# Sparse attention followed by a gated MLP: transposes of the first batch on TensorE, the spatial weight transposed by DMA one batch later

## The chip, the cores and the metric

The kernel runs on one core of one Trainium2 chip. The metric is the device time in microseconds, as the median of the runs. One execution is also recorded by the hardware profiler; where and when below refer to that recording. PE is TensorE, ACT is ScalarE, DVE is VectorE, Pool is GpSimd, and SP is the engine from whose queue nearly all DMAs of this kernel are issued. A queue is worked off in the order of the program.

## What is computed

The reference has two parts. First, block-sparse attention over 4 batches, 8 heads, 768 positions and 64 dimensions a head. Then the heads are put side by side (768 x 512 for each batch) and go through a gated MLP that mixes positions with a 768 x 768 matrix.

```python
# attention (q, k, v: 4 x 8 x 768 x 64); mask: window, first and last block, 3 random blocks a row
scores = scale * np.matmul(q, k.transpose(0, 1, 3, 2))
scores = np.where(mask, scores, -1000000000.0)
attn = softmax(scores)                       # cut: written out in the reference
x = (attn @ v).transpose(0, 2, 1, 3).reshape(4, 768, 512)

# gated MLP (w_in 512 x 1024, w_spatial 768 x 768, w_out 512 x 512)
h = np.maximum(x @ w_in, 0.0)
u, v = h[..., :512], h[..., 512:]
v_n = (v - mean(v)) / np.sqrt(var(v) + 1e-06)
v_s = np.einsum('ts,bsd->btd', w_spatial, v_n) + b_spatial[None, :, None]
out = (u * v_s) @ w_out
```

All inputs are fp32. The kernel casts them to bf16 on the chip.

## The kernel before

The 32 heads are worked on in 16 pairs p, four pairs to a batch, and each pair has 12 slots s. A slot makes the scores of one 128-row chunk of keys of one head (two matmuls), takes their exponential on ACT, and does one sixth of the attention-times-v product of a head 7 slots behind (`LAG = 7`). The MLP of a batch is cut into 24 units (6 v, 6 u, 6 s, 6 o), which are put between the slots of the next batch; those of the last batch run alone at the end.

For matmuls, q and k must have the head dimension on the partitions, and x must have the model dimension there. So each pair's q and k, and each pair's normalised output, are transposed, either on PE (with a copy by DVE out of PSUM) or by a DMA transpose.

```python
def prepare(p):                       # casts on Pool, fp32 -> bf16
    for nm in "kq":
        nat_tile(p, nm)
        cast_qk(p, nm, slice(0, 2), nc.gpsimd)
    cast_v(p)

def tr_pair(p, nm, third):            # transpose of q or k of a pair on PE, two chunks at a time
    if third == 0:
        tr_ps[nm] = psum.tile([128, S], BF16, tag="moe", bufs=2, name="ps_tr")
    ...
    for c in (2 * third, 2 * third + 1):
        nc.tensor.transpose(...)
    if third == 2:
        for h in range(2):
            nc.vector.tensor_copy(out=(qt if nm == "q" else kt)[(2 * p + h) % 4][0:D, :], in_=ps[h * D:(h + 1) * D, :])

def tr_dma(p, nm):                    # the same by DMA ...
    tt[nm, p] = work.tile([128, NCH, 128], BF16, tag=f"tt_{nm}", bufs=2, name=f"tt_{nm}")
    nc.sync.dma_start_transpose(out=tt[nm, p], in_=nat.pop((nm, p)).rearrange("p c h d -> p (c h d)"))

def split_pair(p, nm):                # ... and the split into two heads by DVE
    for h in range(2):
        nc.vector.tensor_copy(...)

def norm(j):                          # attention output of head j, divided by its row sums
    nc.vector.reciprocal(out=rc, in_=ps[:, :, D:VA])
    nc.vector.tensor_tensor(out=xn_ref[p][:, :, h, :], in0=ps[:, :, 0:D], in1=rc.to_broadcast([128, NCH, D]), op=ALU.mult)

def xtr(p):                           # x of a pair, transposed
    if p % NG == NG - 1:              # last pair of a batch: on PE
        ...
    else:
        nc.sync.dma_start_transpose(...)

def wspt_third(i):                    # w_spatial transposed on PE, two chunks at a time
    ...

def v_unit(tcc=tcc):                  # first unit of the MLP; u, s and o units are alike
    ps = moe_ps(last)
    for g in range(NDM):
        nc.tensor.matmul(out=ps, lhsT=xt(g)[...], rhs=w_in_t[:, g, DH:DFF], ...)
    ... relu into vsb, bn_stats, bn_aggr on DVE
    ... for every third unit: rstd on Pool
```

The main loop, cut to what the change touches:

```python
for p in range(NP + 1):
    for s in range(12):
        g = 12 * p + s
        ...
        qk_exp(j, ci)
        ...
        if p + 1 <= NG:                            # NG = 4: pairs 1 to 4 on PE
            first = 4 if p else 6
            if first <= s < first + 3:
                tr_pair(p + 1, "k", s - first)
            elif first + 3 <= s < first + 6:
                tr_pair(p + 1, "q", s - first - 3)
        elif p + 1 < NP and s in (5, 9):
            split_pair(p + 1, "k" if s == 5 else "q")
        if s == 10 and NG < p + 2 < NP:            # pairs 5 to 15 by DMA
            tr_dma(p + 2, "k")
            tr_dma(p + 2, "q")
        if p == 0 and s == 0:
            cast_v(0); prepare(1); load(2); load_weights(3)
        if s == 7 and p + 2 < NP:
            if p + 3 < NP:
                load(p + 3)
            if p < 3:
                load_weights(2)
            prepare(p + 2)
            if p < 4:
                cast_weights((3, 2, 2, 2)[p])
        ... a unit of the MLP, where one is due
        av(ja, qc)
        if qc == NCH - 1:
            norm(ja)
        if p in (2, 3) and not 4 <= s < 10:
            ... wspt_third(...), three in two slots
        if s == 8 and p >= 1:
            xtr(p - 1)
            if p % NG == 0:
                moe_q.extend(moe_units(p // NG - 1))
```

The weights come in nine pieces in the order of a list: three of w_spatial (768 KB each), four of w_in (512 KB each), two of w_out (512 KB each). They are staged in fp32 in buffers that the MLP uses later, and are cast by Pool.

Of the kernel before, what the change touches and what calls it, by code (L numbers as in the profile page):

```python
# [11 lines left out]
BF16 = mybir.dt.bfloat16  # L12
# [14 lines left out]
def kernel(  # L27
# [16 lines left out]
    nc = tc.nc  # L44

    B, H, S, D = q.shape
# [3 lines left out]
    NCH = S // 128  # L50
# [6 lines left out]
    NG = H // 2  # L57
    NP = B * NG
# [5 lines left out]
    work = ctx.enter_context(tc.tile_pool(name="work", bufs=1))  # L64
    psum = ctx.enter_context(tc.tile_pool(name="psum", bufs=1, space=bass.MemoryType.PSUM))
    ctx.enter_context(tc.manual_schedule())

    ident = const.tile([128, 128], BF16)
# [3 lines left out]
    ws_nat = const.tile([128, NCH, S], BF16)  # L72
    w_spt = const.tile([128, NCH, S], BF16)
# [48 lines left out]


    w_pieces = deque()
    for c2 in range(3):
        w_pieces.append((moe_w_spatial.rearrange("(p c) s -> p c s", c=NCH)[:, 2 * c2:2 * c2 + 2],
                         ws_nat[:, 2 * c2:2 * c2 + 2, :]))
    for g in range(NDM):
        w_pieces.append((moe_w_in.rearrange("(g p) f -> p g f", p=128)[:, g:g + 1],
                         w_in_t[:, g:g + 1, :]))  # L130
    for g in range(NDH // 2):
        w_pieces.append((moe_w_out.rearrange("(g p) f -> p g f", p=128)[:, 2 * g:2 * g + 2],
                         w_out_t[:, 2 * g:2 * g + 2, :]))
# [3 lines left out]
    def load_weights(n):  # L137
        for _ in range(n):
            src, dst = w_pieces.popleft()
            a, f = dst.shape[1:]  # L140
            t = work.tile([128, NCH * DH // 2], FP32, tag=w_tags[0], bufs=2,
                          name="wst")[:, 0:a * f].rearrange("p (a f) -> p a f", a=a)
            w_tags.rotate(-1)
            nc.sync.dma_start(out=t, in_=src)
            w_staged.append((t, dst))

    def cast_weights(n):
        for _ in range(n):
            t, dst = w_staged.popleft()
            nc.gpsimd.tensor_copy(out=dst, in_=t)  # L150
# [24 lines left out]
    def keep_warm(n, cols):  # L175
        for _ in range(n):
            nc.tensor.matmul(out=wps[:, 0:cols], lhsT=warm[:, 0:128], rhs=warm[:, 0:cols],
                             start=True, stop=True)
# [43 lines left out]
    def tr_head(h, nm, copy):  # L222
        ps = psum.tile([128, S], BF16, tag="moe", bufs=2)
        for c in range(NCH):
            nc.tensor.transpose(out=ps[0:D, c * 128:(c + 1) * 128], in_=nat[nm, 0][:, c, h],
                                identity=ident)
        copy((qt if nm == "q" else kt)[h][0:D, :], ps[0:D, :])

    tr_ps = {}
# [26 lines left out]
    def mask_rows(sl):  # L256
        nc.vector.tensor_copy(out=kt[sl][D:KR, :], in_=kt[0][D:KR, :])
        nc.vector.tensor_copy(out=qt[sl][D:KR, :], in_=qt[0][D:KR, :])

    def second_head():  # L260
        mask_rows(1)
        cast_qk(0, "k", slice(1, 2), nc.vector)
        cast_qk(0, "q", slice(1, 2), nc.vector)
# [8 lines left out]
    def split_pair(p, nm):  # L272
        src = tt.pop((nm, p)).rearrange("x c n -> x (c n)")
        for h in range(2):
            nc.vector.tensor_copy(out=(qt if nm == "q" else kt)[(2 * p + h) % 4][0:D, :],
                                  in_=src[h * D:(h + 1) * D, :])


    a_ref, av_ref, xn_ref, xt_ref = {}, {}, {}, {}

    def qk_exp(j, ci):
        if ci == 0:
            a_ref[j] = work.tile([128, NCH, S], BF16, tag="a_all", bufs=3, name="a_all")
        ps = psum.tile([128, 1024], FP32, tag="sc", bufs=2)
        for hf in range(2):
            nc.tensor.matmul(out=ps[:, hf * 512:hf * 512 + HALF],  # L286
                             lhsT=kt[j % 4][:, ci * 128:(ci + 1) * 128],
                             rhs=qt[j % 4][:, hf * HALF:(hf + 1) * HALF],
                             start=True, stop=True)
        nc.scalar.activation(  # L290
            out=a_ref[j][:, ci, :].rearrange("p (b c) -> p b c", b=2),
            in_=ps.rearrange("p (b c) -> p b c", b=2)[:, :, 0:HALF],
            func=AF.Exp, scale=0.125)
# [15 lines left out]
    def norm(j):  # L309
        p, h = divmod(j, 2)  # L310
        if h == 0:
# [4 lines left out]
        nc.vector.tensor_tensor(out=xn_ref[p][:, :, h, :], in0=ps[:, :, 0:D],  # L316
                                in1=rc.to_broadcast([128, NCH, D]), op=ALU.mult)

    def xtr(p):
        xn = xn_ref.pop(p)  # L320
        xt_ref[p] = work.tile([128, S], BF16, tag="xt", bufs=8, name="xt")
        if p % NG == NG - 1:
            ps = psum.tile([128, S], BF16, tag="moe", bufs=2)
            for c in range(NCH):
                nc.tensor.transpose(out=ps[:, c * 128:(c + 1) * 128], in_=xn[:, c],
                                    identity=ident)
            nc.vector.tensor_copy(out=xt_ref[p], in_=ps)
        else:
            nc.sync.dma_start_transpose(
                out=xt_ref[p].rearrange("p (c n) -> p c n", c=NCH),  # L330
                in_=xn.rearrange("p c h d -> p (c h d)"))


    ws_ps = {}

    def wspt_third(i):
        sc, third = divmod(i, 3)
        if third == 0:
            ws_ps[0] = psum.tile([128, S], BF16, tag="moe", bufs=2, name="ps_ws")
        ps = ws_ps[0]  # L340
        for tcc in (2 * third, 2 * third + 1):
            nc.tensor.transpose(
                out=ps[:, tcc * 128:(tcc + 1) * 128],
                in_=ws_nat[:, tcc, :].rearrange("p (s c) -> p c s", c=NCH)[:, sc, :],
                identity=ident)
        if third == 2:
            nc.vector.tensor_copy(out=w_spt[:, sc, :], in_=ps)

    tail_tags = deque(["sc", "av", "moe"])

# [109 lines left out]
# [3 lines that stand above are left out]
            j, ci = divmod(g, NCH)  # L463
            if p == NP and g - LAG >= 2 * NP * NCH:
                break
            if p < NP:
                qk_exp(j, ci)
            if p == 0 and s == 0:
                second_head()
            if p == 0 and s < 6:  # L470
                keep_warm(2, 128)
            if p == 0 and s == 3:
                tr_head(1, "k", dve_copy)
            if p == 0 and s == 4:
                tr_head(1, "q", dve_copy)
                mask_rows(2)
                mask_rows(3)
            if p + 1 <= NG:
                first = 4 if p else 6
                if first <= s < first + 3:  # L480
                    tr_pair(p + 1, "k", s - first)
                elif first + 3 <= s < first + 6:
                    tr_pair(p + 1, "q", s - first - 3)
            elif p + 1 < NP and s in (5, 9):
                split_pair(p + 1, "k" if s == 5 else "q")
            if s == 10 and NG < p + 2 < NP:
                tr_dma(p + 2, "k")
                tr_dma(p + 2, "q")
            if p == 0 and s == 0:
                cast_v(0)  # L490
                prepare(1)
                load(2)
                load_weights(3)
            if s == 7 and p + 2 < NP:
                if p + 3 < NP:
                    load(p + 3)
                if p < 3:
                    load_weights(2)
                prepare(p + 2)
                if p < 4:  # L500
                    cast_weights((3, 2, 2, 2)[p])
            if moe_q and slots_left > 0:
                budget += sum(u[0] for u in moe_q) / slots_left
                slots_left -= 1
                while moe_q and budget >= moe_q[0][0] / 2:
                    ns, run = moe_q.popleft()
                    run()
                    budget -= ns
            if g >= LAG:
                ja, qc = divmod(g - LAG, NCH)  # L510
                av(ja, qc)
                if qc == NCH - 1:
                    norm(ja)
            if p in (2, 3) and not 4 <= s < 10:
                for i in range(3 * (s if s < 4 else s - 6) // 2, 3 * (s + 1 if s < 4 else s - 5) // 2):
                    wspt_third(9 * (p - 2) + i)
            if s == 8 and p >= 1:
                xtr(p - 1)
                if p % NG == 0:
                    moe_q.extend(moe_units(p // NG - 1))  # L520
                    slots_left = 48
                    budget = 0.0
# [35 lines left out]
```

The softmax here doesn't subtract the row's maximum and nothing guards it: scores larger than these inputs give would overflow.

## Time and profile before

| | |
|---|---|
| device time, median of 3 | 232.52 us (231.07 to 233.09) |
| the profiled execution | 231.97 us, of it 230.2 us from the first to the last instruction |
| mean granted TensorE clock | 0.991 |
| PE busy | 216.9 us (94%) |
| ACT busy | 171.3 us (74%) |
| DVE busy | 131.5 us (57%) |
| Pool busy | 59.9 us (26%) |
| DMA packets of SP's queue | 39.34 MB, 64.5% of 16 engines' span |

Busy times are of the whole span. The kernel has stages with different limits: the first four pairs run with no MLP beside them, twelve pairs have the MLP of the batch before between their slots, and at the end one MLP runs alone. A share of the whole span says little about each. The page also has the span in 40 slices, the chain of work that ended last, followed back from the last instruction, and groups of instructions with their durations; the trace gives each engine's instructions in order of time, with the idle time before one and what ended it.

Durations that the text uses: a DVE copy of 64 x 768 out of PSUM takes 0.555 us, one of 128 x 768 out of PSUM 0.548 to 0.558 us, one of 64 x 768 from SBUF to SBUF 0.35 us. Pool's cast of 128 x 1536 takes 1.467 us, of 128 x 1024 1.04 us and of 128 x 768 0.83 us.

### The profile page before, as it was taken

Reading aid. Unit: us, or ns where it says so; the run is one execution under the profiler, and the core shown is the slowest. Engines: PE = TensorE matmul, PEld = TensorE weight load, DVE = VectorE, ACT = ScalarE, POOL = GpSimd, SP = SyncE. Lnnn points to the kernel's source line nnn. Section 1 sums busy time; section 2 is a strip of 40 time slices with the busy share of each in tenths; the row PEclk is TensorE's granted clock in tenths of the full one; section 3 lists DMA queues with packets and bytes.
Section 4 is the critical chain, followed back from the end, with each engine's and each line's share of the span. In section 5 each row is a group of like instructions: output and inputs, shape, how many; then the busy total and the mean of one; then the engine's idle time right before and its main releaser. Section 6 shows DMA issues by size and latency. Waiting matters only on the chain.

```text
span 230.2 us, 5333 instructions
## 1 busy us (share of the span) xinstructions
PE 216.9 (94%) x2154; PEld 131.2 (57%) x2154; DVE 131.5 (57%) x285; ACT 171.3 (74%) x245; POOL 59.9 (26%) x88
## 2 busy tenths in 40 slices
PE   7899999948999999999999999999999999999993
PEld 3567777624665555566666555566665555544551
DVE  6664565415997335338995544269992423575532
ACT  5899999953789866796799666987798677257341
POOL 5535775540135401210162401210160000012000
PEclk9999999997999999999999999999999999999999
DMA  6599999999408482999938383999050323520015
GB/s 205 206 293 405 393 325 335 276 174 309 140 17 166 151 125 56 251 256 313 280 66 207 98 118 66 289 270 291 14 103 3 80 48 74 191 92 0 0 48 230
DMA packets 55293, 40.07 MB, mean 174 GB/s; under 512 B 38500, under 2 KB 50788, under 8 KB 55268
## 3 DMA queue, kind: packets, MB, share of 16 engines
q1 hardware_dynamic: 54980, 39.34, 64.5%
q8 instruction: 17, 0.28, 0.5%
q10 hardware_dynamic: 288, 0.39, 0.5%
q14 instruction: 8, 0.07, 0.1%
HBM read 24.38 MB, written 6.29 MB: 133 GB/s over the span
## 4 chain that ended last, share of the span: by engine, by line
PE 71%; DMA 18%; ACT 4%; SPq 3%; DVE 1%; issue 1%; POOL 1%
PE ps L286 19%; PE ps_moe L423 10%; PE ps_av L302 10%; PE ps_moe L378 7%; PE ps_moe L441 7%; PE ps_moe L401 7%; DMA wst<-in_moe_w_in_dram 6%; DMA wst<-in_moe_w_out_dram 4%; ACT a_all L290 4%; DMA tt_k<-nat_k 3%; DMA st_k<-in_k_dram 3%; PE ps_t L423 2%; DMA st_v<-in_v_dram 2%; SPq L95 2%; PE ps_t L378 2%; PE ps_t L441 2%
## 5 line engine op out<-in xcount | busy, mean ns | idle before, releaser
L290 ACT ACTIVATE a_all<-ps 128x768 bf16<-128x768 f32 x192 | 143.1, 812 | 35.3 <-PE ps L286 35.1
L286 PE MATMUL ps<-qt,kt 88*128 88x384 bf16 x384 | 93.9, 325 | 4.3 <-ACT a_all L290 3.1
L302 PEld LDWEIGHTS <-a_all 128*128 128x128 bf16 x1152 | 60.7, 98 | 29.7 <-issue 0.5
L302 PE MATMUL ps_av<-vv,a_all 128*128 128x65 bf16 x1152 | 67.6, 194 | 0.0
L286 PEld LDWEIGHTS <-kt 88*128 88x128 bf16 x384 | 28.7, 98 | 8.2 <-issue 5.2
L426 DVE SCALAR_TENSOR_TENSOR gn<-ps_moe,b_col,un 128x512 bf16<-128x512 f32 x18 | 13.5, 751 | 27.7 <-PE ps_moe L423 27.7
L423 PE MATMUL ps_moe<-vn,w_spt 128*128 128x512 bf16 x108 | 26.3, 378 | 0.0
L112 POOL CAST vv<-st_v 128x768 bf16<-128x768 f32 x16 | 13.4, 840 | 43.2 <-PE ps_av L302 38.6
L391 POOL TENSOR_SCALAR std<-mv 128x3 f32<-128x3 f32 x8 | 1.9, 242 | 77.9 <-DVE mv L388 65.7
L423 PEld LDWEIGHTS <-w_spt 128*128 128x128 bf16 x144 | 13.8, 97 | 14.3
L378 PE MATMUL ps_moe<-w_in_t,xt 128*128 128x512 bf16 x72 | 19.3, 392 | 0.0
L316 DVE TENSOR_TENSOR xn<-ps_av,rc 128x384 bf16<-128x384 f32 x32 | 17.8, 558 | 1.4 <-DVE rc L315 0.3
L109 POOL CAST nat_k<-st_k 128x768 bf16<-128x768 f32 x15 | 12.5, 833 | 23.0 <-issue 11.1
L401 PE MATMUL ps_moe<-w_in_t,xt 128*128 128x512 bf16 x72 | 18.5, 378 | 0.0
L441 PE MATMUL ps_moe<-w_out_t,gt 128*128 128x512 bf16 x72 | 18.5, 378 | 0.0
L387 DVE BATCH_NORM_STATS2 stats<-vsb 128x6 f32<-128x512 bf16 x24 | 16.7, 694 | 1.9 <-ACT vsb L382 1.3
L378 PEld LDWEIGHTS <-xt 128*128 128x128 bf16 x96 | 9.5, 99 | 10.5 <-issue 1.1
L448 DVE COPY osb<-ps_moe 128x512 f32<-128x512 f32 x9 | 6.2, 692 | 15.0 <-PE ps_moe L441 14.9
L401 PEld LDWEIGHTS <-xt 128*128 128x128 bf16 x96 | 9.3, 97 | 9.6
L441 PEld LDWEIGHTS <-gt 128*128 128x128 bf16 x96 | 8.9, 97 | 8.4
L384 DVE TENSOR_SCALAR vsb<-ps_moe 128x512 bf16<-128x512 f32 x18 | 12.3, 682 | 1.9 <-PE ps_moe L378 1.9
L405 DVE TENSOR_SCALAR vn<-vsb,mv,rstd 128x512 bf16<-128x512 bf16 x24 | 12.7, 564 | 0.6 <-POOL rstd L393 0.5
(85 smaller groups left out, 190.0 us busy)
## 6 DMA issues: line engine op xcount, KB each, us to landing
st_v<-in_v_dram SPq DMA_DIRECT2D x16, 384.0 KB, 5.4
out_dram<-osb SPq DMA_DIRECT2D x24, 256.0 KB, 2.5
st_q<-in_q_dram SPq DMA_DIRECT2D x15, 384.0 KB, 4.0
st_k<-in_k_dram SPq DMA_DIRECT2D x15, 384.0 KB, 4.9
wst<-in_moe_w_spatial_dram SPq DMA_DIRECT2D x3, 768.0 KB, 9.1
wst<-in_moe_w_in_dram SPq DMA_DIRECT2D x4, 512.0 KB, 12.1
wst<-in_moe_w_out_dram SPq DMA_DIRECT2D x2, 512.0 KB, 9.8
st_k<-in_k_dram ACTq DMA_DIRECT2D x2, 192.0 KB, 2.9
```

The source lines that it names most:

```text
L112: nc.gpsimd.tensor_copy(out=vv[p % 3][:, :, :, 0:D], in_=st.pop(("v", p)).rearrange("p h (c d) -> p h c d", d=D))
L286: nc.tensor.matmul(out=ps[:, hf * 512:hf * 512 + HALF], lhsT=kt[j % 4][:, ci * 128:(ci + 1) * 128], rhs=qt[j % 4][:, hf * HALF:(hf + 1) * ...
L290: nc.scalar.activation(out=a_ref[j][:, ci, :].rearrange("p (b c) -> p b c", b=2), in_=ps.rearrange("p (b c) -> p b c", b=2)[:, :, 0:HALF], ...
L302: nc.tensor.matmul(out=av_ref[j][:, qc, :], lhsT=a_ref[j][:, ci, qc * 128:(qc + 1) * 128], rhs=vv[p % 3][:, h, ci, :], start=(ci == 0), st ...
L316: nc.vector.tensor_tensor(out=xn_ref[p][:, :, h, :], in0=ps[:, :, 0:D], in1=rc.to_broadcast([128, NCH, D]), op=ALU.mult)
L378: nc.tensor.matmul(out=ps, lhsT=xt(g)[:, tcc * 128:(tcc + 1) * 128], rhs=w_in_t[:, g, DH:DFF], start=(g == 0), stop=(g == NDM - 1))
L387: nc.vector.bn_stats(out=stats, in_=vsb[:, tcc, :])
L401: nc.tensor.matmul(out=ps, lhsT=xt(g)[:, tcc * 128:(tcc + 1) * 128], rhs=w_in_t[:, g, 0:DH], start=(g == 0), stop=(g == NDM - 1))
L405: nc.vector.tensor_scalar(out=vn[:, tcc, :], in0=vsb[:, tcc, :], scalar1=mv[:, tcc, 0:1], scalar2=rstd[:, tcc:tcc + 1], op0=ALU.subtract, ...
L423: nc.tensor.matmul(out=ps, lhsT=w_spt[:, sc, tcc * 128:(tcc + 1) * 128], rhs=vn[:, sc, :], start=(sc == 0), stop=(sc == NCH - 1))
L426: nc.vector.scalar_tensor_tensor(out=gn[:, tcc, :], in0=ps, scalar=b_col[:, tcc:tcc + 1], in1=un[:, tcc, :], op0=ALU.add, op1=ALU.mult)
L441: nc.tensor.matmul(out=ps, lhsT=gt[:, tcc, dhc, :], rhs=w_out_t[:, dhc, :], start=(dhc == 0), stop=(dhc == NDH - 1))
```

## The change

Four things are done at once.

- q and k of pair 5 are transposed on PE as those of pairs 1 to 4 are. In pairs 1 to 4 these transposes move from slots 4 to 9 to slots 0 to 5.
- x of pairs 0, 1 and 2 (the first batch) is transposed on PE in thirds, in slots 8 to 10 of the following pair. So no DMA transpose is issued in the first batch at all.
- w_spatial is no longer transposed on PE. Pool's cast, which reads the staged fp32 rows, reads every sixth element and so writes the columns in the order in which chunks of 128 are wanted; then six DMA transposes of 128 x 768 make the transposed matrix. Its loads move from the start to pairs 3 and 4, its casts to pair 4, its transposes to pairs 5 and 6.
- w_in is now loaded first, and w_out in pair 5, with its casts in pair 6.

The purpose is to take DMA work out of the first batch, where all loads of weights and the transposes come together.

```diff
     w_pieces = deque()
-    for c2 in range(3):
-        w_pieces.append((moe_w_spatial.rearrange("(p c) s -> p c s", c=NCH)[:, 2 * c2:2 * c2 + 2],
-                         ws_nat[:, 2 * c2:2 * c2 + 2, :]))
     for g in range(NDM):
         w_pieces.append((moe_w_in.rearrange("(g p) f -> p g f", p=128)[:, g:g + 1],
                          w_in_t[:, g:g + 1, :]))
+    for c2 in range(3):
+        w_pieces.append((moe_w_spatial.rearrange("(p c) s -> p c s", c=NCH)[:, 2 * c2:2 * c2 + 2],
+                         ws_nat[:, 2 * c2:2 * c2 + 2, :].rearrange(
+                             "p t (c s) -> p t c s", c=NCH)))
 ... in load_weights:
+            if len(dst.shape) == 4:
+                t = t.rearrange("p a (s c) -> p a c s", c=NCH)
 ... x:
+    def xtr_third(p, third):
+        if third == 0:
+            xt_ref[p] = work.tile([128, S], BF16, tag="xt", bufs=8, name="xt")
+            tr_ps["x"] = psum.tile([128, S], BF16, tag="moe", bufs=2, name="ps_x")
+        ps = tr_ps["x"]
+        for c in (2 * third, 2 * third + 1):
+            nc.tensor.transpose(out=ps[:, c * 128:(c + 1) * 128], in_=xn_ref[p][:, c],
+                                identity=ident)
+        if third == 2:
+            xn_ref.pop(p)
+            nc.vector.tensor_copy(out=xt_ref[p], in_=ps)
 ... w_spatial (wspt_third is gone):
+    def wspt(tcc):
+        nc.sync.dma_start_transpose(out=w_spt[:, :, tcc * 128:(tcc + 1) * 128],
+                                    in_=ws_nat[:, tcc, :])
 ... the loop:
-            if p + 1 <= NG:
-                first = 4 if p else 6
+            if p <= NG:
+                first = 0 if p else 6
 ...
-            if s == 10 and NG < p + 2 < NP:
+            if s == 10 and NG + 1 < p + 2 < NP:
                 tr_dma(p + 2, "k")
                 tr_dma(p + 2, "q")
             if p == 0 and s == 0:
 ...
-                load_weights(3)
+                load_weights(2)
             if s == 7 and p + 2 < NP:
                 if p + 3 < NP:
                     load(p + 3)
-                if p < 3:
-                    load_weights(2)
+                if p in (0, 3, 4, 5):
+                    load_weights((2, 0, 0, 2, 1, 2)[p])
                 prepare(p + 2)
-                if p < 4:
-                    cast_weights((3, 2, 2, 2)[p])
+                if p in (0, 1, 4, 6):
+                    cast_weights((2, 2, 0, 0, 3, 0, 2)[p])
 ...
-            if p in (2, 3) and not 4 <= s < 10:
-                for i in range(3 * (s if s < 4 else s - 6) // 2, 3 * (s + 1 if s < 4 else s - 5) // 2):
-                    wspt_third(9 * (p - 2) + i)
-            if s == 8 and p >= 1:
+            if p in (NG + 1, NG + 2) and s in (0, 3, 6):
+                wspt(3 * (p - NG - 1) + s // 3)
+            if 1 <= p < NG and 8 <= s < 11:
+                xtr_third(p - 1, s - 8)
+            if s == 8 and p >= NG:
                 xtr(p - 1)
```

More of the change, by code (lines that the diff above doesn't have):

```diff
@@ L139, in load_weights @@
             src, dst = w_pieces.popleft()
-            a, f = dst.shape[1:]
+            a, f = src.shape[1:]
             t = work.tile([128, NCH * DH // 2], FP32, tag=w_tags[0], bufs=2,
@@ L317, in norm @@
                                 in1=rc.to_broadcast([128, NCH, D]), op=ALU.mult)
+    def xtr_third(p, third):
[9 more added lines that the diff above has]
+            nc.vector.tensor_copy(out=xt_ref[p], in_=ps)
     def xtr(p):
-        xn = xn_ref.pop(p)
-        xt_ref[p] = work.tile([128, S], BF16, tag="xt", bufs=8, name="xt")
         if p % NG == NG - 1:
[L323 to L327, printed above, removed]
-        else:
+            for third in range(3):
+                xtr_third(p, third)
+        else:
+            xn = xn_ref.pop(p)
+            xt_ref[p] = work.tile([128, S], BF16, tag="xt", bufs=8, name="xt")
             nc.sync.dma_start_transpose(
@@ L331, in xtr @@
                 in_=xn.rearrange("p c h d -> p (c h d)"))
[L334 to L347, printed above, removed]
+    def wspt(tcc):
+        nc.sync.dma_start_transpose(out=w_spt[:, :, tcc * 128:(tcc + 1) * 128],
+                                    in_=ws_nat[:, tcc, :])
     tail_tags = deque(["sc", "av", "moe"])
```

## The prediction

> **What bounds the kernel now.** I read the page's 40 slices first. Two engines matter there, and DMA:
>
> ```profile
> PE   7899999948999999999999999999999999999993
> ...
> ACT  5899999953789866796799666987798677257341
> ...
> PEclk9999999997999999999999999999999999999999
> DMA  6599999999408482999938383999050323520015
> ```
>
> A slice is 230.2/40 = 5.76 us. ACT is full up to slice 7 (46 us), while the first batch's attention runs alone; from slice 9 on PE is full and ACT is not. Between them, slice 8 (46 to 52 us), PE falls to 4, and the granted clock dips in the slice after. Busy times by stretch say the same:
>
> ```profile
> 20.00:30.00 10.00, 9.95 (x142) 7.75 (x141) 5.14 (x11) 10.00 (x15) 8.08 (x8) 1.00 1.04 395
> 30.00:40.00 10.00, 10.00 (x148) 7.94 (x147) 6.69 (x15) 10.00 (x15) 6.71 (x8) 1.00 1.13 323
> ...
> 46.00:52.00 6.00, 2.55 (x32) 1.67 (x30) 0.92 (x4) 3.33 (x5) 2.43 (x3) 1.00 1.33 181
> 52.00:56.00 4.00, 3.49 (x21) 1.93 (x22) 1.96 (x5) 0.81 (x1) 0.00 (x0) 0.57 1.13 303
> 56.00:66.00 10.00, 10.00 (x104) 6.04 (x103) 9.31 (x21) 7.67 (x11) 1.12 (x2) 1.00 0.41 130
> ```
>
> Columns: window, length, busy time of PE, weight load, DVE, ACT, POOL, then PE clock, DMA share, GB/s. From 20 to 40 us ACT is busy 10.00 of 10. From 46 to 52 nobody is busy but DMA (share 1.33, yet only 181 GB/s). The chain that ended last shows what holds it:
>
> ```profile
> 33.09 10.18 DMA wst<-in_moe_w_out_dram
> 43.46 7.55 DMA tt_k<-nat_k
> 51.04 0.35 DVE kt L275
> 51.40 0.36 DVE kt L275
> 51.90 0.57 DVE xn L316
> 52.51 0.82 PE ps L325 x6
> ```
>
> Start, length, what. The DMA transpose of pair 5's k takes 7.55 us, behind w_out and other transposes; the two DVE copies that split it sit in DVE's queue ahead of the norm of the last head of batch 0; xtr(3) on PE waits for that norm. PE's timeline gives the size of the hole:
>
> ```profile
> 47.98 0.48 PE L286 MATMUL ps<-qt,kt 88*128 88x384 bf16 x2
> 48.30 0.36 PE L302 MATMUL ps_av<-vv,a_all 128*128 128x65 bf16 x6
> 52.51 0.82 PE L325 MATMUL ps<-ident,xn 128*128 128x128 bf16 x6 [3.85 <-DVE xn L316]
> 53.13 0.85 PE L286 MATMUL ps<-qt,kt 88*128 88x384 bf16 x2
> 53.77 1.87 PE L378 MATMUL ps_moe<-w_in_t,xt 128*128 128x512 bf16 x4
> 55.47 0.36 PE L302 MATMUL ps_av<-vv,a_all 128*128 128x65 bf16 x6
> 55.66 0.49 PE L286 MATMUL ps<-qt,kt 88*128 88x384 bf16 x2
> ```
>
> PE is idle 3.85 us, then works at half speed to about 55.5: four 512-column matmuls take 1.87 us, against 1.03 in the following units. I number slots 12p+s. Slot 12's scores start at 16.30 us and slot 56's at 47.98: 44 slots of 0.72 us, exactly ACT's pace (nine exps in 6.47 us). From slot 58 (55.66 us) on PE sets the pace: two slots with one v-unit take 1.9 us.
>
> **What the skill says.** The Trainium skill, "TensorE: Matmul & The Clock Gate", Part 1 (architectural detail), calls ACT and DVE "strict FIFO". The trace agrees: a ready norm stood behind a copy that waited 7.3 us. The same page, Part 1 (clock gate), says an idle PE window of about 3.4 us halves the clock until another window of work has passed; here 3.85 us of idling were followed by 0.50 granted in the 53 to 55 us windows and 1.00 from 56 us. "GPSIMD Engine Reference", section 7, says a read whose element step exceeds 8 bytes costs some 2.9 cycles an element instead of 1.9. The permuting cast reads fp32 with a step of 24 bytes; no instruction of the trace before has such a read. The contiguous cast of the same size takes 1.467 us.
>
> **The change, part by part.**
>
> *q and k of pair 5 on PE.* Removed: two DMA transposes (7.55 us to land for k, issue times 1.85 and 3.96 us) and four DVE copies of 0.35 us. Added: 12 PE transposes and four DVE copies from PSUM of 0.555 us. They lie in slots 48 to 53, two transposes a slot. Pairs 2 to 4 already do this in their slots, and the trace keeps 0.70 to 0.75 us a slot there, so it lies beside ACT: path cost 0. The wait that made the hole no longer exists.
>
> *x of pairs 0 to 2 on PE.* Three DMA transposes go, 18 PE transposes and three DVE copies of 0.55 us come, in slots 8 to 10 of pairs 1 to 3. The norm they need is emitted in slot 6 of that pair, and takes about 1.0 us (0.20 + 0.56 and a 0.3 us gap), against 1.44 us to slot 8: just enough. Path cost 0.
>
> *w_spatial off PE.* 36 PE transposes and six DVE copies (0.558 us each, 3.3 us) leave pairs 2 and 3. Both were under ACT's exps, so gain 0 on the path. In all PE has 36 - 18 - 12 = 6 transposes fewer, all in the ACT-bound part.
>
> *DMA.* w_spatial's 2.3 MB and w_out's 1.0 MB leave the first 40 us; at the 395 GB/s of the 20 to 30 us window that is 8.5 us of DMA. No DMA transpose is issued before pair 4 slot 10, so SP runs ahead: q, k of pair 6, w_spatial and pair 6's transposes should be issued around 30 to 42 us instead of 37 to 54 (estimate: their staging buffers come free with casts that are no longer late).
>
> *Batch 1.* w_spatial's three casts stand behind v of pair 6 on Pool, which needs the last av of pair 3 (slot 54, 47 us). At 1.467 us times 2.9/1.9 = 2.2 us each (estimate from the skill's ratio) they run from about 47.7 to 54.5; at 3.7 us (2.9 cycles at the page's 1.2 GHz, also an estimate) to 59. The first DMA transpose of w_spatial is meant for slot 60, about 52 us after the change, and each costs SP about 1.2 us and lands in 2.8, as the undisturbed x transposes do. The first s-unit comes 21 slots into batch 0's MoE, slot 77, about 71 us. Even with the slow estimate some 9 us are to spare. w_out is cast in pair 6 and first used near slot 93.
>
> *Sum.* Slot 56 still starts at 47.98. Then 0.32 for its scores, 0.20 for av (48.5), six transposes 0.4 (48.9; the norm has been ready since about 48.1), scores of slot 57 0.33, v-unit 0.86 (50.1, perhaps 0.1 to 0.2 more for the copy of x), av 0.20: slot 58 starts at 50.3 to 50.5 instead of 55.66. That is 5.2 to 5.4 us: 3.85 of idling and about 1.4 of half clock. After it PE is the bound in both kernels with the same instructions, so the whole shift reaches the end: 232.5 - 5.3 = 227.2. The profiled execution (231.97) lay 0.5 below the median, so the hole in the median run may be a little longer; I say 227.0.
>
> **Rivals.**
>
> *The hole moves to pair 6.* Its k and q are still transposed by DMA, and their split copies sit on DVE in slots 65 and 69. If their transposes were to queue behind w_spatial's loads and pair 7's, norm and av would again stall. Against it: issued by about 42 us and needed at 57; in the trace before, even 7.55 us to land would do. If true, 1 to 3 us come back: 228 to 230.
>
> *Pool becomes the holder.* If a strided cast takes 5 us or more, three of them end after 63 us; rstd for batch 0 and pair 7's casts stand behind them, and DVE waits at the first vn (60.6 us). DVE is already 9.31 of 10 busy in the v-units, and its SBUF copies slow down while Pool works: the split copies of q at 67.6 us took 1.38 us for two instead of 0.71. For it: no strided cast is in the trace. Against it: vn isn't needed before slot 77, so some 5 us can be absorbed. If true, 1 to 3 us lost: 228 to 230.
>
> *ACT-bound, so nothing moves.* If the hole were hidden by ACT, taking it away would win nothing: 232. Against it: ACT itself idled 4.68 us in the hole, and the chain passes through PE right after it.
>
> *An early PE wait.* Pair 2's k is now needed at slot 12 (16.6 us), and its cast ends at 16.43 in the trace. A few tenths of delay would go straight into ACT's chain: 227.3 to 227.6.
>
> **Range and chances.** The core of the sum is two durations read off one stretch, so I hold 225.5 to 229.0 with 8 in 10: down 1.5 for a longer hole in the median run, up 2 for half of a rival. Over 2% means below 227.87. My centre is 0.9 under that, the scatter of the runs before is 2 us, and any rival eats the margin: 0.71 faster, 0.26 same, 0.03 slower.
>
> **What would show it.** Right: no PE idle above 1 us and no clock dip between 46 and 56 us; xtr(3) on PE near 48.5; the first v-unit near 49.3; slot 56 still near 48.0; the chain without tt_k and without w_out. Strided casts of 2 to 4 us ending before 60; w_spatial's transposes landed before slot 77. Wrong: PE waiting for xn, or DVE for tt_k, near slots 65 to 70; s-units waiting for w_spatial; DVE waiting for rstd; or ACT idle before 46 us, which would mean that the transposes of x or of pair 2 came too early.

## The result

The changed kernel takes 226.46 us (226.41 to 226.99, 4 runs) against 232.59 us before: a ratio of 0.975, with a 95% interval of 0.971 to 0.980. The prediction was 227.0 us, in a range of 225.5 to 229.0.

The profile after, in the slices that answer to those shown of before:

```profile
PE   7889999999999999999999999999999999999993
...
ACT  5899999988898677877898668877898666266351
...
PEclk9999999999999999999999999999999999999999
DMA  5689979977997985999365665998050424610016
```

Slice 8 of PE is full, and the granted clock never dips. Busy times by stretch (columns as before: window, length, PE, weight load, DVE, ACT, Pool, clock, DMA share, GB/s):

```profile
46.00:52.00 6.00, 5.92 (x72) 3.96 (x71) 4.04 (x9) 5.40 (x8) 4.90 (x3) 1.00 0.51 52
52.00:56.00 4.00, 4.00 (x46) 2.45 (x43) 3.83 (x9) 3.10 (x5) 4.00 (x2) 1.00 1.05 123
56.00:66.00 10.00, 10.00 (x100) 5.87 (x99) 9.65 (x21) 8.77 (x13) 6.63 (x10) 1.00 1.00 280
```

From 46 to 52 us PE is busy 5.92 us of 6, where it was 2.55; Pool, busy 2.43 us there before with the casts of pair 6, now has 4.90 us, most of it the casts of w_spatial. PE's timeline at the place of the hole:

```profile
47.80 0.48 PE L289 MATMUL ps<-qt,kt 88*128 88x384 bf16 x2
48.12 0.36 PE L305 MATMUL ps_av<-vv,a_all 128*128 128x65 bf16 x6
48.31 0.50 PE L328 MATMUL ps_x<-ident,xn 128*128 128x128 bf16 x6
...
48.98 1.03 PE L379 MATMUL ps_moe<-w_in_t,xt 128*128 128x512 bf16 x4
...
50.03 0.49 PE L289 MATMUL ps<-qt,kt 88*128 88x384 bf16 x2
```

The transposes of x follow the av matmuls at once. Slot 58's scores start at 50.03 us instead of 55.66, which is 5.63 earlier, and the span is 230.2 - 224.6 = 5.6 us shorter. So the whole difference arises before slot 58, and on balance nothing is won or lost after it.

### The profile page after: what moved, and what is told of

Its sections match the earlier page's. It is cut to its first block, busy times and chain, and to the rows that moved or that the text cites. A ratio compares the mean times of both kernels' runs of the same rounds, so it can differ in the third digit from the quotient of the medians.

```text
span 224.6 us, 5315 instructions
## 1 busy us (share of the span) xinstructions
PE 215.3 (96%) x2148; PEld 130.5 (58%) x2148; DVE 131.2 (58%) x282; ACT 171.1 (76%) x245; POOL 64.0 (28%) x88
## 4 chain that ended last, share of the span: by engine, by line
PE 79%; ACT 17%; DVE 1%; issue 1%
PE ps L289 22%; ACT a_all L293 17%; PE ps_av L305 11%; PE ps_moe L424 10%; PE ps_moe L379 7%; PE ps_moe L442 7%; PE ps_moe L402 7%; PE ps_t L424 2%; PE wps L180 2%; PE ps_t L379 2%; PE ps_t L442 2%; PE ps_t L402 2%; PE ps_sc L424 1%; PE ps L228 1%; PE ps_sc L442 1%
## 5 line engine op out<-in xcount | busy, mean ns | idle before, releaser
L392 POOL TENSOR_SCALAR std<-mv 128x3 f32<-128x3 f32 x8 | 1.9, 241 | 65.2 <-DVE mv L389 53.9
L402 PE MATMUL ps_moe<-w_in_t,xt 128*128 128x512 bf16 x72 | 18.5, 378 | 0.0
L379 PE MATMUL ps_moe<-w_in_t,xt 128*128 128x512 bf16 x72 | 18.5, 378 | 0.0
```

Of the source, the lines that this page charges most:

```text
L379: nc.tensor.matmul(out=ps, lhsT=xt(g)[:, tcc * 128:(tcc + 1) * 128], rhs=w_in_t[:, g, DH:DFF], start=(g == 0), stop=(g == NDM - 1))
L402: nc.tensor.matmul(out=ps, lhsT=xt(g)[:, tcc * 128:(tcc + 1) * 128], rhs=w_in_t[:, g, 0:DH], start=(g == 0), stop=(g == NDM - 1))
```

## Experiments

The recorded executions differ by up to 1.7 us before the first exp on ACT, where the kernels do nearly the same work (the kernel before and run 6, whose edit lies near slot 56: 7.30 and 8.90 us). Six transposes take 0.85 us at the start of run 6 and 0.52 in the kernel before, so PE's clock opens later there. The runs below are therefore also compared by the time from the first exp to the end, which is the span less the start of the first exp in the profile. That is one execution a kernel, so a few tenths of a microsecond say little. Each ratio is to executions of the kernel before made along with that run (medians of 232.3 to 232.9 us), and is not the quotient of two lines of the table.

| kernel | device time, us | ratio to before (95%) | span | first exp | from first exp to end |
|---|---|---|---|---|---|
| before | 232.59 | | 230.2 | 7.30 | 222.9 |
| changed | 226.46 | 0.975 (0.971 to 0.980) | 224.6 | 7.30 | 217.3 |
| 1: before, pair 5 on PE | 227.39 | 0.981 (0.974 to 0.988) | 225.5 | 7.25 | 218.2 |
| 2: before, w_out late | 228.42 | 0.984 (0.977 to 0.991) | 226.8 | 7.97 | 218.8 |
| 3: changed, pair 5 by DMA | 229.84 | 0.989 (0.987 to 0.992) | 228.3 | 7.16 | 221.1 |
| 4: changed, x by DMA | 226.88 | 0.978 (0.971 to 0.984) | 225.2 | 7.88 | 217.3 |
| 5: changed, w_spatial on PE in batch 1 | 230.34 | 0.990 (0.985 to 0.995) | 229.8 | 8.90 | 220.9 |
| 6: before, PE kept busy in the hole | 231.48 | 0.994 (0.991 to 0.996) | 230.2 | 8.90 | 221.3 |
| 7: changed, permuting casts twice | 232.69 | 0.999 (0.997 to 1.001) | 230.3 | 7.90 | 222.4 |
| 8: changed, pair 1 a slot earlier | 226.51 | 0.976 (0.972 to 0.979) | 224.6 | 7.32 | 217.3 |
| 9: before, split copies after the norm | 228.57 | 0.980 (0.976 to 0.985) | 227.1 | 7.92 | 219.2 |
| 10: as 7, casts cut in six | 239.38 | 1.029 (1.025 to 1.034) | 236.4 | 7.62 | 228.8 |
| 11: as 3, q copied two slots earlier | 230.94 | 0.995 (0.992 to 0.997) | 229.3 | 8.09 | 221.2 |
| 12: before, pair 5 on PE and w_out late | 227.30 | 0.978 (0.974 to 0.983) | 225.7 | 7.92 | 217.8 |

### What made the hole

**1. Pair 5 on PE, alone.**

```diff
-            if p + 1 <= NG:
-                first = 4 if p else 6
+            if p <= NG:
+                first = (0 if p == NG else 4) if p else 6
-            if s == 10 and NG < p + 2 < NP:
+            if s == 10 and NG + 1 < p + 2 < NP:
```

> The kernel before, with one part of the change alone: q and k of pair 5 are transposed on PE in slots 0 to 5 of pair 4, and their two DMA transposes and four split copies are gone. All else (w_spatial on PE in pairs 2 and 3, w_out's load in pair 2, x by DMA) as before. Theory A (the hole was only the split copies of pair 5 standing ahead of the norm): the hole and the dip of the clock vanish, slot 58 starts near 50.3 us instead of 55.7, the time is 226.5 to 227.8. Rival B (the early DMA traffic is the cause, and would show up at the next user of a DMA transpose): a wait of 1 us or more appears at pair 6's split copies or at a v-unit that waits for x, and the time is 229 or more.

The hole is gone: 4.7 of the 5.6 us come from this part alone. A short wait stays at the first v-unit, on PE's timeline of this kernel:

```profile
50.03 0.61 PE L378 MATMUL ps_moe<-w_in_t,xt 128*128 128x512 bf16 x2 [0.33 <-DMA xt<-xn]
```

It waits for the DMA transpose of x of pair 2, which SP issued at 40.96 us, behind w_out. So rival B holds in small: the early DMA traffic shows up at the next reader of a DMA transpose, for half a microsecond.

**2. w_out late, alone.**

```diff
-                if p < 3:
+                if p in (0, 1, 5):
                     load_weights(2)
...
-                if p < 4:
-                    cast_weights((3, 2, 2, 2)[p])
+                if p in (0, 1, 2, 6):
+                    cast_weights((3, 2, 2, 0, 0, 0, 2)[p])
```

> The kernel before, with w_out's two loads moved from pair 2 to pair 5 and its casts to pair 6, and nothing else. Pair 5 stays on DMA. If w_out's 1 MB is what delays pair 5's k (about 2.7 us at 390 GB/s), it lands about 2.7 us earlier, the hole shrinks from 3.9 to 1 or 2 us, too short for the clock to drop, and the time is 228.5 to 229.5. If the x transposes and the pair's own transposes are what keeps the DMA queue, w_out changes little: 231.5 to 232.7.

The first theory holds, and a little more comes back than it said (228.42 us against 228.5 to 229.5): with pair 5 still on DMA, moving 1 MB of loads away wins 4.1 us from the first exp to the end. PE's timeline:

```profile
50.15 0.51 PE L325 MATMUL ps<-ident,xn 128*128 128x128 bf16 x6 [0.82 <-DVE xn L316]
```

The idle time is 0.82 us instead of 3.85, and the six transposes take 0.51 us, so the clock did not drop.

**9. Only the order on DVE.**

```diff
-            elif p + 1 < NP and s in (5, 9):
-                split_pair(p + 1, "k" if s == 5 else "q")
+            elif p + 1 < NP and s in ((9, 11) if p == NG else (5, 9)):
+                split_pair(p + 1, "k" if s == (9 if p == NG else 5) else "q")
```

> The kernel before, with only the place of pair 5's split copies changed in DVE's order: k in slot 9 and q in slot 11 of pair 4 instead of 5 and 9, so that the norm of the last head of batch 0 (slot 6) and the copy of x stand ahead of them. The DMA transposes are as late as before. If the order in DVE's queue made the hole, PE passes slot 56 without a wait, DVE waits for k from about 49.5 to 51 us, under the two PSUM buffers of the v-units, and the time is 226.8 to 228.5. If the late transpose itself is what counts, q and k of pair 5 are then late for slot 60 and the time is 230 or more.

Not a byte moves earlier here; two pairs of DVE copies go behind the norm. The time, 228.57 us, is just above what was expected (226.8 to 228.5); from the first exp it is 3.7 us shorter than before. PE passes slot 56 without a wait and waits 0.46 us for x of pair 2 and 0.53 us for q of pair 5 later. So the loss needed two things together: a late transpose, and its reader ahead of the norm on a first-in first-out engine. Runs 1 and 2 take away the first, run 9 the second, and each recovers about two thirds or more of the 5.6 us.

**6. The clock's share.**

```diff
+            if s == 8 and p == NG:
+                wps2 = psum.tile([128, 512], FP32, tag="moe", bufs=2, name="wps2")
+                for _ in range(17):
+                    nc.tensor.matmul(out=wps2, lhsT=warm[:, 0:128], rhs=warm, start=True, stop=True)
             if s == 8 and p >= 1:
                 xtr(p - 1)
```

> The kernel before, with 17 matmuls of 512 columns on a zero tile put on PE ahead of the transposes of x of pair 3 (about 3.7 us of work whose result nobody reads), so that PE is busy through the hole and its clock does not drop. The wait itself stays. If the half clock after the hole costs 1.4 us by itself, the time falls from 232.6 to 231.0 to 231.5 and slot 58 starts near 54.3 us. If the loss is the wait alone, nothing changes: 232 or more.

PE is busy in the hole with matmuls whose result nobody reads, by its timeline:

```profile
49.73 0.48 PE L286 MATMUL ps<-qt,kt 88*128 88x384 bf16 x2
...
50.46 3.62 PE L520 MATMUL wps<-warm 128*128 128x512 bf16 x16
53.91 0.50 PE L325 MATMUL ps<-ident,xn 128*128 128x128 bf16 x6
...
55.63 0.49 PE L286 MATMUL ps<-qt,kt 88*128 88x384 bf16 x2
```

In this execution PE started 1.6 us late, so k of pair 5 came sooner in the count of slots; the norm was ready at 51.8 us and the dummy matmuls themselves held PE until 53.9. What the run does show is the stretch from the x transposes to slot 58's scores with a stop of about the same length ahead of it (3.5 us of dummy matmuls), but without idling: 55.63 - 53.91 = 1.72 us, the same as in the changed kernel (50.03 - 48.31). Before, it was 55.66 - 52.51 = 3.15 us. So 1.4 us of the loss were half clock. The time of the whole run, 231.48 us, is in the expected range, but it mixes this with the late start and shows little by itself.

**3, 4 and 12. Which parts are needed.**

Run 12 is run 1 and run 2 together. Runs 3 and 4 are the changed kernel with one part undone:

```diff
 run 3
-            if p <= NG:
+            if p < NG:
                 first = 0 if p else 6
-            if s == 10 and NG + 1 < p + 2 < NP:
+            if s == 10 and NG < p + 2 < NP:
 run 4
-            if 1 <= p < NG and 8 <= s < 11:
-                xtr_third(p - 1, s - 8)
-            if s == 8 and p >= NG:
+            if s == 8 and p >= 1:
                 xtr(p - 1)
```

> The changed kernel, with q and k of pair 5 back on DMA transposes (issued in pair 3, slot 10; split copies in pair 4, slots 5 and 9). Loads and x as in the changed kernel. Theory A (either half of the change suffices: with no x transposes and no weights before it, pair 5's transpose is issued as soon as its cast is done, near 34 to 40 us, and lands by 44, before its copies are due at about 46): same time as the changed kernel, 226.2 to 227. Rival B (PE transposes for pair 5 are what matters): a hole again, 229 or more.

> The changed kernel, with x of pairs 0 to 2 transposed by DMA as before. Pair 5 stays on PE, weights stay late. Theory: nobody waits for these three transposes before the first v-unit, so the time is that of the changed kernel, 226.2 to 227.2, and x on PE is not part of the gain. Rival: in SP's queue they wait for their norms and hold the loads behind them, k of pairs 4 to 6 is cast late, and PE or DVE waits for it: 227.5 or more.

> The kernel before, with pair 5 on PE and w_out's loads and casts late; w_spatial stays on PE in pairs 2 and 3, x of the first batch stays on DMA. If these two parts are the whole gain, 217.2 to 217.7 us from the first exp to the end, as in the changed kernel (218.2 with pair 5 alone, whose first v-unit waited 0.5 us for x of pair 2). If w_spatial off PE brings something in the first batch, 218 or more.

Run 4: x by DMA costs nothing once the weights are late (217.3, as the changed kernel). Run 12: the two parts give 217.8, so 5.1 of the 5.6 us. That lies between the two expectations (up to 217.7, or from 218). w_spatial's early load and transposes account for a part of the rest in that execution: ACT lost 0.28 us near 27.5 us, where PE's weight load waited 0.3 us for a cast of w_spatial. Half a microsecond on single profiles is little to build on.

Run 3 was a surprise. Theory A expected 226.2 to 227, and it took 3.8 us more from the first exp. Yet the hole had not come back: the x transposes start at 48.30 us with no wait. PE waits later, and the chain of waits of this kernel names what for:

```profile
50.03 1.00 DVE qt L278
...
51.06 2.98 DVE qt L278
54.04 0.61 DVE vsb L385
...
54.70 1.44 PE ps_moe L379 x4
```

A DVE copy of q that takes 0.35 us elsewhere takes 2.98 us. Its data had landed long before. In that time Pool runs the permuting casts, by its timeline. The first line has all three; then come the first of them alone and the first copy of q:

```profile
47.85 8.97 POOL L153 CAST ws_nat<-wst 128x1536 bf16<-128x1536 f32 x3
...
47.85 2.96 POOL L153 CAST ws_nat<-wst 128x1536 bf16<-128x1536 f32 x1
...
49.31 1.72 DVE L278 COPY qt<-tt_q 64x768 bf16<-64x768 bf16 x1
```

What PE loses by it comes in two terms, as in the hole: it stops for 1.77 us ahead of the v-unit at 54.70, and from 55.5 to 58.5 us its granted clock is 0.50. From that v-unit to the scores that follow the next one it takes 4.58 us, against 2.96 in the changed kernel: 1.6 us more.

### A copy beside a cast

**7. The casts done twice.**

```diff
             t, dst = w_staged.popleft()
-            nc.gpsimd.tensor_copy(out=dst, in_=t)
+            for _ in range(2 if len(dst.shape) == 4 else 1):
+                nc.gpsimd.tensor_copy(out=dst, in_=t)
```

> The changed kernel, with each of the three permuting casts of w_spatial done twice on Pool (same result; a doubled cost). They then run from 47.9 to about 65.6 us instead of 56.7. Theory (some 5 us of slack on Pool, since vn is first needed at slot 77): DVE waits for rstd from about 61.7 to 66.9, but PE waits little: 226.4 to 227.2. Rival (Pool is close to being the holder): 228 or more.

The theory of 5 us of slack falls: from the first exp it takes 5.1 us more than the changed kernel, as much as the change had won. The same two copies of pair 6's k, in DVE's timeline, first in the changed kernel and then here:

```profile
57.31 0.69 DVE L278 COPY kt<-tt_k 64x768 bf16<-64x768 bf16 x2
```

```profile
57.92 5.63 DVE L279 COPY kt<-tt_k 64x768 bf16<-64x768 bf16 x2
63.47 0.68 DVE L386 TENSOR_SCALAR vsb<-ps_moe 128x512 bf16<-128x512 f32 x1
```

DVE stands 5.63 - 0.69 = 4.9 us longer. PE's timeline shows what comes of it:

```profile
64.20 0.59 PE L403 MATMUL ps_moe<-w_in_t,xt 128*128 128x512 bf16 x1 [3.55 <-DVE vsb L386]
```

PE stops for 3.55 us, and from 64 to 67 us its granted clock is 0.50; from this u-unit to the second scores after it (67.15) it takes 2.95 us, against 1.58 in the changed kernel. The stop and these 1.4 us make nearly the whole loss. In the changed kernel the casts ran from 47.87 to 56.6 us and the copies started at 57.31: the margin on DVE was 0.7 us, not 5. The other work of DVE in the same time is not slowed (bn_stats 0.69 us, the relu out of PSUM 0.68, as elsewhere). The Trainium skill, "GPSIMD Engine Reference", section 8, says that GpSimd shares its SBUF interfaces with VectorE, and contends with DVE instructions in a 2-port mode or with two SBUF inputs. The trace agrees that instructions from SBUF to SBUF suffer, and gives the size: not a slower rate, but a stop until a cast has ended. In run 3 the first cast ends at 50.82 us and the copy caught beside it at 51.03; the second cast takes 3.07 us and ends at 53.82, the second copy at 54.04. The caught copies of runs 7 and 11 also end 0.21 to 0.23 us after a cast. So does one in the changed kernel, beside a contiguous cast that ends at 63.14: it takes from 62.35 to 63.35 us.

**11. q copied two slots earlier than in run 3.**

```diff
-            elif p + 1 < NP and s in (5, 9):
+            elif p + 1 < NP and s in ((5, 7) if p == NG else (5, 9)):
                 split_pair(p + 1, "k" if s == 5 else "q")
```

> The kernel with pair 5 back on DMA, with only its split copies of q moved from slot 9 to slot 7 of pair 4, so that they run before Pool starts the permuting casts at 47.9 us. Theory C: the 4.7 us that the two copies took beside the casts fall to 0.7, and from the first exp to the end it takes 217.2 to 217.8 us, as in the changed kernel (221.1 with the copies in slot 9). Rival (pair 5 on DMA costs time by itself): 219 or more.

This did not do what it was meant to. DVE reached the copies at 48.57 us, after the norm; Pool's casts began at 48.67, and one of the two copies was caught again:

```profile
48.57 3.37 DVE L278 COPY qt<-tt_q 64x768 bf16<-64x768 bf16 x2
```

Being caught in front of the copy of x, it cost as much as before: PE stops for 1.89 us, by the profile for the copy of x, and then has half the clock. The 221.2 us lie in the rival's range (219 or more). That pair 5 by DMA costs nothing without the collision is thus argued from run 3's trace (no wait at slot 56, all of the loss at these copies), and not shown by a time.

**10. The same Pool work in small pieces.**

```diff
+            if len(dst.shape) == 4:
+                for _ in range(2):
+                    for a in range(2):
+                        for c in range(0, NCH, 2):
+                            nc.gpsimd.tensor_copy(out=dst[:, a, c:c + 2], in_=t[:, a, c:c + 2])
 ... else, the other weights' casts as before
```

> The kernel of the doubled casts (each permuting cast of w_spatial twice), with each cast cut into six pieces of 256 columns, so that Pool does the same work in 36 instructions of about 0.5 us instead of 6 of 2.96 us. New theory C (a DVE copy from SBUF to SBUF cannot run beside a Pool instruction and waits for the end of the one in flight): each of the two copies of pair 6's k now waits 0.5 us or less instead of 2.8, PE sees no wait, and from the first exp to the end it takes 217.3 to 218.5 us (222.4 with the whole casts, 217.3 in the changed kernel). Rival D (Pool's total load, or rstd and pair 7's casts behind it, is what holds): 221 to 223.

Theory C, that a copy waits for the end of the Pool instruction in flight, fits every caught copy beside whole casts, but falls here: it is much worse. DVE's and Pool's timelines of this kernel:

```profile
57.63 11.59 DVE L284 COPY kt<-tt_k 64x768 bf16<-64x768 bf16 x1
```

```profile
48.20 20.82 POOL L157 CAST ws_nat<-wst 128x256 bf16<-128x256 f32 x36
69.10 0.23 POOL L398 TENSOR_SCALAR std<-mv 128x3 f32<-128x3 f32 x1
```

One copy stood from 57.63 to 69.22 us, until the last of 36 casts without a gap had ended at 69.02; some twenty ends of Pool instructions passed it by. The casts of 0.634 us start every 0.58 us, so each begins on record before the one ahead has ended. That doesn't explain it: in run 3 the second cast begins at 50.75 us and the first ends at 50.82, and in the changed kernel the contiguous casts from 62.31 us on overlap in the same way (the first ends at 63.14, the second begins at 63.08), and yet copies got in at these boundaries. Why a boundary was passed over in one and used in the other is not settled. What holds in runs 3, 7, 10 and 11 is that a run of Pool casts can stop an SBUF-to-SBUF copy on DVE for 3 to 12 us. Rival D's range (221 to 223) is missed as well.

### Two other sizes

**5. w_spatial on PE in batch 1.** Cast in its own order, then for each of six chunks, in slots 62 to 72:

```diff
-            if p in (NG + 1, NG + 2) and s in (0, 3, 6):
-                wspt(3 * (p - NG - 1) + s // 3)
+            if 62 <= g <= 72 and g % 2 == 0:
+                wspt((g - 62) // 2)
 ... cut: wspt is now six PE transposes and one DVE copy out of PSUM
```

> The changed kernel, with w_spatial cast in its own order (no step of 24 bytes) and transposed on PE in batch 1: six times six PE transposes and a DVE copy of 0.56 us, in slots 62 to 72, instead of the six DMA transposes. In batch 1 PE sets the pace, so the 36 transposes should show in full: six of them take PE about 0.34 to 0.40 us, in all 2.0 to 2.4 us, and the time is 228.5 to 229.2; if DVE, over 9 of 10 busy in the v-units, holds PE back as well, 229.5 to 231. If PE had room in batch 1, under 227. The three casts should take 1.47 us each, against 2.96.

From the first exp it takes 220.9 us, 3.6 more than the changed kernel: above what PE's transposes alone explain (six times 0.34 us is 2.0). The time, 230.34 us, is in the range of the second branch, which put the rest down to DVE. That isn't shown: PE's one longer wait there, 0.54 us ahead of the transposes at 64.54, is put down to ACT by the profile. The three casts take 4.29 us in all, so 1.43 each against 2.92 for the permuting ones by the same count. Moving w_spatial late is only free because its transposes also leave PE.

**8. Pair 1 a slot earlier.**

```diff
-                first = 0 if p else 6
+                first = 0 if p else 5
```

> The changed kernel, with the transposes of pair 1's k and q one slot earlier (slots 5 to 10 of pair 0 instead of 6 to 11). In the changed kernel's trace the scores of slot 12 wait 0.45 us for the copy of pair 1's q, and ACT waits 0.43 us after it. If that wait goes straight into ACT's chain, the time from the first exp to the end falls from 217.3 to 216.8 to 217.0 us. If the copies of the mask rows that stand ahead on DVE, or the cast of k, take its place: no change.

No change (217.3). The wait for q is gone from slot 12, and another stands in its place on PE's timeline:

```profile
16.64 0.28 PE L239 MATMUL ps_tr<-ident,nat_k 128*128 128x128 bf16 x2 [0.37 <-POOL nat_k L109]
```

It is the cast of pair 2's k, which the prediction had named as a near miss. No run beat the changed kernel.

## Why the prediction was right

*The idle time and the half clock.* Predicted 3.85 and about 1.4 us. Measured from where the x transposes follow slot 56's av, 0.2 us after its start: 52.51 - 48.50 = 4.0 us of stop, and 3.15 - 1.72 = 1.4 us of half clock; together 5.4, plus 0.18 us by which slot 56 itself came earlier (47.80 against 47.98). Runs 1, 2, 6 and 9 show both terms and the cause that the chain had named.

*The transposes on PE in the first batch lie beside ACT.* Right: slots 12 to 56 took 31.5 us in the changed kernel (16.30 to 47.80) against 31.7.

*All of the shift reaches the end.* Right: 5.63 us at slot 58, 5.6 in the span.

*Early PE wait for pair 2's k.* It did not appear in the changed kernel, but run 8 shows that it stood next in line.

*The hole moving to pair 6.* It did not. Its transposes were issued at 40.11 and 41.53 us, as estimated, and were long done at slot 65. A trace of this rival stands one pair later, where nothing depends on it: DVE waits 1.29 us for the transpose of pair 7's k (copied at 68.22 us), and PE doesn't notice.

*w_spatial's transposes.* Three of the six are issued only from 65.76 us on, behind pair 7's, and each of the six takes 2.7 to 4.2 us to land; so the last ones, issued at 68.42 and 69.74, landed after the first s-unit had begun (70.78), where all had been expected before it. No s-unit waited, as each reads only its own block of 128 columns.

*The idling that halves the clock.* The prediction names an idle window of about 3.4 us. In the kernel before, that fits, but runs 3 and 11 show the same drop after stops of 1.77 and 1.89 us, each with 0.50 granted for about 3.4 us. A stop of 0.82 us (run 2) was not followed by one.

*Pool as the holder.* Here a step was wrong, though it did not touch the time. The cast's size was estimated well: 2.957 us, between the 2.2 and 3.7 that the skill's figures gave; against the contiguous 1.467 it is 2.0 times, more than the page's ratio of 1.5. But "some 5 us can be absorbed" looked at rstd and vn alone. The slack was set by the split copies of pair 6's k on DVE: had the casts ended more than 0.7 us later, DVE would have stood. The prediction had quoted the slowed copies (1.38 us for two) and read them as a small tax; they are a stop that lasts until a cast beside them ends, so it grows with the cast. At 3.7 us a cast, within its own estimate, the casts would have ended near 59 us and held those copies for some 1.7 us (an estimate: 59.0 less 57.3). In run 7 PE stopped 1.35 us less than DVE stood (4.9 less 3.55), so little of that would have reached PE. The range would have held, but not for the reason given; that the casts ended just ahead of the copies was luck.

## What to carry to other kernels

Look for what stands behind a late transfer on a first-in first-out engine: here a DVE copy that nobody needed for another seven slots held a norm that PE needed at once, and changing the order, the traffic or the route each recovered most of the loss. When casts move to Pool, list the SBUF-to-SBUF copies that DVE has in the same stretch: here the slack began with their distance to the casts, and not with the first reader of a Pool result. Cutting such casts into pieces did not let the copies through.

## What was not expected of the hardware

- A 0.35 us DVE copy from SBUF to SBUF took 2.98 us beside a cast of 3.07 us, and 11.59 us beside a row of 36 casts of 0.63 us without gaps. The DVE instruction that writes vn, also from SBUF to SBUF, took 0.80 to 0.96 us instead of 0.41 beside contiguous casts (63.38 to 66.61 us of the changed kernel). DVE instructions that read PSUM, and bn_stats, were not slowed.
- PE's granted clock fell to 0.50 for about 3.4 us after stops of 1.77 us (run 3) and 1.89 us (run 11).
- A Pool cast that reads fp32 with a step of 24 bytes takes 2.957 us for 128 x 1536, 2.0 times the 1.467 us of the contiguous one.
- The start of PE's full clock varies between executions and moves the first exp, from 7.16 to 8.90 us. Before the change a part of that came back: transfers do not start later with it, so the hole is shorter when PE is late, as in run 6.
